# A local score bank's mask as two 64-column products, and pieces of row transposes and gate at other places of the attention steps

## The chip, the cores and the metric

The kernel runs on one core of one Trainium2 chip. Its five engines (TensorE, VectorE, ScalarE, GpSimd and SyncE; PE, DVE, ACT, POOL and SP in the profile) each work through a list of instructions of their own, in order, and wait for each other with semaphores. The metric is the device time of one execution in microseconds. Before the change three runs gave 695.32, 699.48 and 699.75 us, with a median of 699.48 us.

## The reference

The reference is window attention over 8 batches and 8 heads, and a mixture of experts over its output rows. A sequence has 32 global and 512 local positions with 64 numbers per head. Global queries see all 544 keys; a local query sees the 32 global keys and the local keys at most 32 positions away.

```
s_g = scale * q_g @ k_all.T ;  out_g = sm(s_g) @ v_all
s_ll = where(|pos_q - pos_k| <= 32, scale * q_l @ k_l.T, -1e9)
a_l  = sm(concat([scale * q_l @ k_g.T, s_ll]))
out_l = a_l @ concat([v_g, v_l])
x = concat([out_g, out_l]) with the heads side by side: 8 x 576 rows of 512
for each row in order: e = argmax(x @ w_gate), or the row before's e if sigmoid(x @ w_local) >= 0.5
out = softmax(x @ w_gate)[e] * (relu(x @ w1[e]) @ w2[e])
```

## The kernel before

The attention comes first and takes about the first 243 us of the profiled execution. Two heads (a pair) are worked on together. `run` walks over 48 units, six for each batch, in the order local pair 0, local pair 1, global 0, local pair 2, global 1, local pair 3. The step of a unit `nx` does its scores, and the transposes and the value product of the unit two steps earlier, `st`. So a step is one of six kinds, by the kinds of `nx` and `st`; they come round once a batch:

- `nx` local 0, `st` global 1 of the batch before
- `nx` local 1, `st` local 3 of the batch before
- `nx` global 0, `st` local 0
- `nx` local 2, `st` local 1
- `nx` global 1, `st` global 0
- `nx` local 3, `st` local 2

A local unit has two score banks (`hb` 0 and 1), each one PSUM bank of 128 x 512. `l_s` fills a bank: one bf16 product of the identity with a table (`mask`) writes 0 or -8e9 into 256 of its columns, then eight fp32 products add the scores (L243). Each of these eight has 64 stationary columns, and they write rows 0 to 63 and rows 64 to 127 of the bank by turns. `l_max` (VectorE, L248 and L250) takes the row maximum and writes the difference into `pe`, `l_exp` (ScalarE, L254) makes its exponential, `l_t` (L260) transposes it on TensorE with ScalarE copying it out (L262), and `l_av` (L276) multiplies it with the values in products of 32 stationary columns. `g_s`, `g_max`, `g_exp`, `g_t` and `g_av` do the same for a global unit.

TensorE thus works with three shapes of its stationary operand: 128 columns (every transpose, and the mask product), 64 columns (L243 and the global scores L296) and 32 columns (`l_av`, `g_av` L339, the gate products L367, L375, L388). The profile writes them as 128*128, 128*64 and 128*32.

The rest of a batch is a list of pieces, `fin`, of which `fpiece` does one: `f1` (four transposes L352 of a finished 128 columns of the attention output, copied to `xT` by ScalarE, L353), `f1g` (the same for the global rows, L359), `f2` and `f2g` (gate products), `f3` (transposes of the gate). A step calls `fpiece` at two places. The pieces due are the same in every batch from the second on: in the step of local 0 it is `f1` of pair 2 of the batch before, in that of local 1 its `f1g`, in that of global 0 its `f2g` and the `f1` of its pair 3, in that of local 2 its `f2` and `f3`, in that of global 1 `f1` of this batch's pairs 0 and 1, and in that of local 3 none.

Buffers that matter here: score banks are a ring of four PSUM banks (ps0 to ps3), transposes of all kinds go through a ring of two (ps4 and ps5, `ps_t`), value and gate products through another ring of two (ps6 and ps7, `ps_o`). The program order is the order of the code; no scheduler moves anything. Between the pieces of VectorE's work `drip` puts single instructions of the routing (`keys`, `probs`, `stage_a`).

After the attention come `tail` and the experts (`Moe`), which the change doesn't touch: the products L1251 and L1262 over weights loaded by SyncE, in the order of the experts.

Of the kernel before, what the change touches and what calls it, by code (L numbers as in the profile page):

```python
# [18 lines left out]
P = 128  # L19
# [80 lines left out]
class Attn:  # L100
# [125 lines left out]
    def l_s(self, st, hb):  # L226
        nc = self.nc
        if hb == 0:
            b, pr = st["u"]
            if pr == 0:  # L230
                self.cur[b]["xa"] = self.xa()
                self.cur[b]["xg"] = self.xg()
            st["pe"] = self.pe()
        qbd = st["qbd"]
        kf = st["kx"].rearrange("p m c k -> p (m c k)")
        sp = st["sp"] = self.bank(self.ps_s)
        mo = sp.rearrange("p t (k c) -> p t k c", c=32)[:, :, 0::3, :]
        nc.tensor.matmul(mo, self.cst.idb, self.mask[:, 4 * hb:4 * hb + 4], start=True, stop=False, skip_group_check=True)
        for t in range(4):
            for t2 in range(2):  # L240
                w = 8 * hb + 2 * t + t2
                f = 32 * (3 * (w // 2) + w % 2)
                nc.tensor.matmul(sp[64 * t2:64 * t2 + 64, t], qbd[:, w], kf[:, f:f + P], start=False, stop=True, skip_group_check=True)  # L243
# [176 lines left out]
    def run(self, rt, moe):  # L420
        order = []
        for b in range(B):
            order += [("l", b, 0), ("l", b, 1), ("g", b, 0), ("l", b, 2), ("g", b, 1), ("l", b, 3)]
        units = [{"k": k, "u": (b, i)} for k, b, i in order]
        pairs = [u for u in units if u["k"] == "l"]
        n = len(units)
        fin = []
        when = []

        def fpiece():  # L430
            if fin and when[0] <= s:
                f, a = fin.pop(0)
                when.pop(0)
                if f is not None:
                    f(*a)
        nc = self.nc
        for k in range(2):
            self.load(*pairs[k]["u"])
        self.load_g(0)
        self.loadv(*pairs[0]["u"])  # L440
        self.cst.ident()
        warm = self.ps_o()[:, 0:P]
        for _ in range(8):
            nc.tensor.matmul(warm, self.cst.idf, self.cst.idf, start=True, stop=True)
        nc.gpsimd.memset(self.pg.t[0], 0.0)
        self.blank(0)
        self.make_mask()
        self.prep(pairs[0])
        self.blank(1)
        nc.vector.memset(self.pg.t[1], 0.0)  # L450
        npr, late = 0, None
        for s in range(n):
            nx = units[s]
            st = units[s - 2] if s >= 2 else None
            nl = nx["k"] == "l"
            sl = st is not None and st["k"] == "l"
            sg = st is not None and not sl
            if nl:
                if npr + 2 < len(pairs):
                    b, i = pairs[npr + 2]["u"]  # L460
                    self.load(b, i)
                    if i == 0:
                        self.load_g(b)
                if npr + 1 < len(pairs):
                    self.loadv(*pairs[npr + 1]["u"])
                npr += 1
                if npr < len(pairs):
                    self.prep(pairs[npr])
            if sl:
                self.l_t(st, 0)  # L470
                self.l_t(st, 1)
            if sg:
                self.g_t(st)
            if late is not None:
                self.l_exp(late, 1)
                late = None
            if nl:
                self.l_s(nx, 0)
                self.l_max(nx, 0)
            else:  # L480
                self.g_s(nx)
                self.g_max(nx)
            fpiece()
            if sl:
                self.l_av(st, 0)
            if nl:
                self.l_exp(nx, 0)
                self.l_s(nx, 1)
                self.l_max(nx, 1)
            fpiece()  # L490
            if not nl:
                self.g_exp(nx)
            if sl:
                self.l_av(st, 1)
            if sg:
                self.g_av(st)
            if nl:
                if s in DEFER:
                    late = nx
                else:  # L500
                    self.l_exp(nx, 1)
            if s == 0:
                self.cst.load()
                self.cst.rest()
                self.gens += [self.setup(), rt.setup()]
            if s < 6:
                self.drip(4)
            moe.pre(s - n)
            if st is not None:
                b, i = st["u"]  # L510
                if sl:
                    fin.append((self.f1, (b, i)))
                    if i == 3:
                        fin += [(self.f2, (b,)), (self.f3, (b, rt))]
                elif i == 1:
                    fin += [(self.f1g, (b,)), (None, ()), (self.f2g, (b,))]
            if len(fin) > 4:
                fpiece()
            when += [s + 1] * (len(fin) - len(when))
        self.drip(1000)  # L520
        moe.tail = self.tail(units[n - 2], units[n - 1], fin, rt, moe)
# [1049 lines left out]
```

## Time and profile before

| | us |
|---|---|
| median of three runs | 699.48 |
| profiled execution | 698.19 |
| its span, first to last instruction | 696.5 |
| TensorE busy (share of the span) | 671.7 (96%) |
| VectorE busy | 427.4 (61%) |
| ScalarE busy | 342.6 (49%) |
| GpSimd busy | 196.2 (28%) |
| mean granted TensorE clock | 0.990 |

The profiled execution is one run of its own, with 1.7 us around its span. A row of the timeline has the start and the length of a run of equal instructions on one engine, both in us, then engine, line, operation, what is written and read, the shape, and the count. TensorE's products are pipelined: a product's row is longer than the time after which the next one may start, so rows overlap, and costs are read from starts. PEld is the loading of a stationary operand, which can go on beside products.

### The profile page before, as it was taken

To read this page: it belongs to the slowest core of one execution; us is meant where nothing else is said; L and a number is where in the kernel's file an instruction comes from. 1 tells how busy PE (TensorE), PEld (TensorE's weight loads), DVE (VectorE), ACT (ScalarE), POOL (GpSimd) and SP (SyncE) were. 2 spreads that over 40 slices of the span, in tenths; PEclk is the share of its full clock that TensorE was granted. 3 is DMA by queue.
4 is the path that set the end of the run, shared out by engine and by line. 5 is a ranking of instruction groups with operands and counts; after the bars stand their busy time and mean duration, and the time that the engine had idled before them with its cause. 6 is when DMAs were issued, how large, how long until landed. Compare 5 with 4: busy or idle time off the path is not lost.

```text
span 696.5 us, 18391 instructions
## 1 busy us (share of the span) xinstructions
PE 671.7 (96%) x7253; PEld 564.2 (81%) x7253; DVE 427.4 (61%) x1057; ACT 342.6 (49%) x614; POOL 196.2 (28%) x321
## 2 busy tenths in 40 slices
PE   9999999999899899998997999999999999999995
PEld 7777777777677787897886898889898989888994
DVE  7878777678887777995516645426353516345563
ACT  4555555655454674652326535334444425255563
POOL 7634344243333301032013303031304021032033
PEclk9999999999999999999999999999999999999998
DMA  8956967866846497776517666428385417265673
GB/s 331 387 213 238 353 235 274 311 240 226 309 181 262 140 353 247 257 230 238 191 60 257 200 219 200 145 76 257 126 260 158 159 66 235 67 211 179 234 259 112
DMA packets 43014, 151.46 MB, mean 217 GB/s; under 512 B 7965, under 2 KB 9245, under 8 KB 38688
## 3 DMA queue, kind: packets, MB, share of 16 engines
q1 hardware_dynamic: 35536, 126.92, 51.5%
q0 software_dynamic: 6960, 21.90, 9.8%
q8 instruction: 77, 1.26, 0.7%
q14 instruction: 153, 1.25, 0.5%
q10 hardware_dynamic: 288, 0.13, 0.1%
HBM read 130.55 MB, written 19.69 MB: 216 GB/s over the span
## 4 chain that ended last, share of the span: by engine, by line
PE 59%; DVE 3%; issue 1%; ACT 1%; POOL 0%; DVEq 0%; ACTq 0%; POOLq 0%
PE ps L1262 28%; PE ps L1251 26%; PE ps L1205 3%; DVE wp L1160 1%; DVE wq L1160 1%; PE ps L1374 0%; DVE xT L991 0%; PE ps L999 0%; POOL xa L1191 0%; DVE xT L989 0%; DVE hl L1254 0%; DVE wp L1208 0%; PE ps L276 0%; PE ps L1363 0%; DVE xl L1160 0%
## 5 line engine op out<-in xcount | busy, mean ns | idle before, releaser
L1268 POOL DMA_INDIRECT out_dram<-y,tk x39 | 40.5, 1039 | 320.0 <-ACT y L1267 257.0
L1262 PE MATMUL ps<-wp,wq 128*128 128x512 f32 x504 | 128.0, 401 | 0.9 <-ACT wq L1365 0.9
L1262 PEld LDWEIGHTS ps<-wp,wq 128*128 128x128 f32 x504 | 93.2, 190 | 20.5 <-ACT wq L1365 1.1
L1251 PE MATMUL ps<-wp,wp 128*128 128x256 f32 (+6 forms) x672 | 107.8, 320 | 0.0
L1251 PEld LDWEIGHTS ps<-wp,wp 128*128 128x128 f32 x672 | 103.4, 189 | 3.6
L1254 DVE SCALAR_TENSOR_TENSOR wq<-ps,wq 128x256 fp32r<-128x256 f32 (+6 forms) x80 | 41.3, 519 | 71.8 <-ACT wq L1253 71.6
L191 POOL TENSOR_SCALAR_AFFINE_SELECT qbd<-raw 64x512 f32<-64x512 f32 x62 | 44.6, 719 | 119.5 <-PE ps L243 100.6
L1208 DVE TENSOR_TENSOR wp<-ps,wp 128x512 fp32r<-128x512 f32 x40 | 27.4, 690 | 80.0 <-ACT wp L1207 80.0
L1253 ACT ACTIVATE wq<-ps 128x256 fp32r<-128x256 f32 (+6 forms) x80 | 36.8, 463 | 77.3 <-PE ps L1251 69.6
L243 PE MATMUL ps<-kx,qbd 128*64 128x128 f32 x1024 | 71.4, 281 | 1.8 <-issue 1.7
L243 PEld LDWEIGHTS ps<-kx,qbd 128*64 128x64 f32 x1024 | 55.1, 137 | 12.7 <-issue 8.3
L1267 ACT ACTIVATE y<-ps,pp 128x512 f32<-128x512 f32 x39 | 26.9, 689 | 76.4 <-PE ps L1262 70.8
L248 DVE TENSOR_REDUCE mx<-ps 128x4 f32<-128x512 f32 x64 | 43.9, 686 | 29.3 <-PE ps L243 29.3
L1160 DVE TENSOR_TENSOR wp<-raw,wp 128x1024 fp32r<-128x1024 f32 x47 | 56.9, 1216 | 2.5 <-ACT wp L1150 2.5
L254 ACT ACTIVATE pe<-pe 128x512 f32<-128x512 f32 x64 | 40.7, 636 | 32.9 <-DVE pe L250 32.9
L1191 POOL DMA_INDIRECT xa<-xs,idx x42 | 51.3, 1220 | 17.1 <-issue 10.0
L1150 ACT CAST wp<-raw 128x1024 fp32r<-128x1024 f32 x49 | 50.7, 1045 | 1.3 <-DMA raw<-in_w_dram 0.5
L1207 ACT CAST wp<-ps 128x512 fp32r<-128x512 f32 x40 | 23.4, 588 | 55.4 <-PE ps L1205 55.4
L250 DVE TENSOR_TENSOR pe<-ps,mx 128x512 f32<-128x512 f32 x64 | 44.0, 688 | 1.6
L276 PE MATMUL ps<-v,pt 128*32 128x65 f32 x2048 | 42.7, 222 | 2.1 <-DVE xa L284 0.8
L276 PEld LDWEIGHTS ps<-v,pt 128*32 128x32 f32 x2048 | 33.3, 110 | 13.8 <-issue 6.7
L191 POOL TENSOR_SCALAR_AFFINE_SELECT kx<-raw 128x384 f32<-128x384 f32 (+3 forms) x127 | 42.7, 369 | 3.0 <-DMA raw<-in_qk_dram 0.9
(279 smaller groups left out, 1173.0 us busy)
## 6 DMA issues: line engine op xcount, KB each, us to landing
raw<-in_w_dram SPq DMA_DIRECT2D x78, 512.0 KB, 3.9
v<-in_vw_dram SPq DMA_DIRECT2D x32, 1040.0 KB, 9.9
raw<-in_qk_dram SPq DMA_DIRECT2D x32, 528.0 KB, 8.2
xa<-in_w_dram SPq DMA_DIRECT2D x26, 512.0 KB, 5.0
xT<-in_w_dram SPq DMA_DIRECT2D x20, 512.0 KB, 4.1
xs<-xa SPq DMA_DIRECT2D x8, 1056.0 KB
qgb<-in_qg_dram SPq DMA_DIRECT2D x8, 128.0 KB
xa<-xs,idx POOLq DMA_INDIRECT x42
```

Source lines behind the costliest of these rows:

```text
L191: self.nc.gpsimd.affine_select(out=out, in_=in_, pattern=pat, compare_op=ALU.is_ge, fill=0.0, base=0, channel_multiplier=0)
L243: nc.tensor.matmul(sp[64 * t2:64 * t2 + 64, t], qbd[:, w], kf[:, f:f + P], start=False, stop=True, skip_group_check=True)
L248: nc.vector.tensor_reduce(out=mx, in_=st["sp"], axis=AX.X, op=ALU.max)
L250: nc.vector.tensor_tensor(out=st["pe"][:, 4 * hb:4 * hb + 4], in0=st["sp"], in1=mx.broadcast_to([P, 4, P]), op=ALU.subtract)
L254: self.nc.scalar.activation(out=pe, in_=pe, func=AF.Exp, scale=SCALE)
L276: nc.tensor.matmul(o[32 * w4:32 * w4 + 32, g, h], pt[:, 2 * g + w4 // 2, w4 % 2, h, :], v[:, w, h * (D + 1):(h + 1) * (D + 1)], start=True ...
L1150: nc.scalar.copy(out=hi, in_=raw)
L1160: (nc.gpsimd if pool else nc.vector).tensor_tensor(out=lo, in0=raw, in1=hi.bitcast(F32), op=ALU.subtract)
L1191: self.nc.gpsimd.indirect_dma_start(out=self.xr[j] if k == "early" else self.xr4[:, j], out_offset=None, in_=src, in_offset=bass.IndirectO ...
L1251: nc.tensor.matmul(ph, a[:, dc, fs], b_[:, dc, n0:n1], start=(n == 0), stop=(n == 11))
L1254: nc.vector.scalar_tensor_tensor(out=hl[:, fc, n0:n1], in0=ph, scalar=0.0, in1=hh[:, fc, n0:n1].bitcast(F32), op0=ALU.max, op1=ALU.subtract)
L1262: nc.tensor.matmul(py, a[:, fc, js], b_[:, fs], start=(fc == 0 and k == 0), stop=(fc == 7 and k == 2))
```

## The change

The mask product becomes two products, one with columns 0 to 63 of the identity into rows 0 to 63 of the bank, the other with columns 64 to 127 into rows 64 to 127. Each has 64 stationary columns and moves the same 256 columns of the table. `fpiece` keeps its two calls per step; where they stand now depends on the kinds of `nx` and `st`.

```diff
         mo = sp.rearrange("p t (k c) -> p t k c", c=32)[:, :, 0::3, :]
-        nc.tensor.matmul(mo, self.cst.idb, self.mask[:, 4 * hb:4 * hb + 4], start=True, stop=False, skip_group_check=True)
+        for r in (slice(0, 64), slice(64, P)):
+            nc.tensor.matmul(mo[r], self.cst.idb[:, r], self.mask[:, 4 * hb:4 * hb + 4], start=True, stop=False, skip_group_check=True)
...
             else:
                 self.g_s(nx)
                 self.g_max(nx)
-            fpiece()
+            if sl:
+                fpiece()
+            if not nl:
+                fpiece()
             if sl:
                 self.l_av(st, 0)
             if nl:
                 self.l_exp(nx, 0)
                 self.l_s(nx, 1)
                 self.l_max(nx, 1)
-            fpiece()
+            if nl:
+                fpiece()
+                if sg:
+                    fpiece()
             if not nl:
+                if sg:
+                    fpiece()
                 self.g_exp(nx)
```

For the steps with `nx` and `st` both local, or both global, the order of the pieces is the same as before. It differs in two of the six kinds of steps. The diff adds lines, so line numbers behind it are one or more higher in the changed kernel (L238 is L239, L243 is L244, L352 is L353).

In the step of local 0, on TensorE, where the third batch begins, there stood this before (ps1 and ps2 are the unit's two score banks, xa1 the attention output of the batch before, ptg1 the transposed global part):

```order
L328 MATMUL ps4_67<-idf_81,pg1_149 128x128 x3
L238 LDWEIGHTS idb_82
L238 MATMUL ps1_64<-mask_154,idb_82 128x4x2x32
L243 MATMUL ps1_64<-kx0_146,qbd0_144 64x128 x8
L352 MATMUL ps5_68<-idf_81,xa1_109 128x128 x4
L238 LDWEIGHTS idb_82
L238 MATMUL ps2_65<-mask_154,idb_82 128x4x2x32
L243 MATMUL ps2_65<-kx0_146,qbd0_144 64x128 x8
L339 MATMUL ps7_70<-v1_133,ptg1_151 32x65 x2
```

And this stands at the same place in the changed kernel:

```order
L329 MATMUL ps4_67<-idf_81,pg1_149 128x128 x3
L239 LDWEIGHTS idb_82
L239 MATMUL ps1_64<-mask_154,idb_82 64x4x2x32
L239 LDWEIGHTS idb_82
L239 MATMUL ps1_64<-mask_154,idb_82 64x4x2x32
L244 MATMUL ps1_64<-kx0_146,qbd0_144 64x128 x8
L239 LDWEIGHTS idb_82
L239 MATMUL ps2_65<-mask_154,idb_82 64x4x2x32
L239 LDWEIGHTS idb_82
L239 MATMUL ps2_65<-mask_154,idb_82 64x4x2x32
L244 MATMUL ps2_65<-kx0_146,qbd0_144 64x128 x8
L353 MATMUL ps5_68<-idf_81,xa1_109 128x128 x4
```

The transposes of `f1` have moved from between the unit's two score banks to behind the second one; the two banks now follow each other. The same moves ScalarE's copy of these transposes. Before, from this step into the next (pe2 is the new unit's score tile, pt2 and pt3 the next step's transposed scores):

```order
L329 COPY ptg1_151<-ps4_67 128x384
L254 ACTIVATE pe1_138<-pe1_138 128x512
L353 COPY xT_112<-ps5_68 128x512
L254 ACTIVATE pe2_139<-pe2_139 128x512
L262 COPY pt2_142<-ps4_67 128x512
L262 COPY pt3_143<-ps5_68 128x512
```

And in the changed kernel:

```order
L330 COPY ptg1_151<-ps4_67 128x384
L255 ACTIVATE pe1_138<-pe1_138 128x512
L255 ACTIVATE pe2_139<-pe2_139 128x512
L354 COPY xT_112<-ps5_68 128x512
L263 COPY pt2_142<-ps4_67 128x512
L263 COPY pt3_143<-ps5_68 128x512
```

The copy to `xT` now stands behind the exponential of the new unit's first bank, and it still frees ps5 for the second four transposes of the next step. Seven batches have this step with an `f1`. In the step of global 0, on TensorE, before (xgT1 feeds the global gate product, v3 the values):

```order
L296 MATMUL ps2_65<-raw1_78,qgb0_152 64x288
L375 MATMUL ps6_69<-xgT1_117,wgg_84 32x32 x4
L276 MATMUL ps7_70<-v3_135,pt0_140 32x65 x16
L352 MATMUL ps5_68<-idf_81,xa1_109 128x128 x4
L276 MATMUL ps6_69<-v3_135,pt1_141 32x65 x16
```

And in the changed kernel:

```order
L297 MATMUL ps2_65<-raw1_78,qgb0_152 64x288
L376 MATMUL ps6_69<-xgT1_117,wgg_84 32x32 x4
L353 MATMUL ps5_68<-idf_81,xa1_109 128x128 x4
L277 MATMUL ps7_70<-v3_135,pt0_140 32x65 x16
L277 MATMUL ps6_69<-v3_135,pt1_141 32x65 x16
```

Here `f1` has moved ahead of both value products. VectorE, GpSimd and SyncE have the same instructions in the same order as before.

## The prediction

> **What bounds the kernel now.** I read the page's first lines, then busy times by stretches of the attention stage, where the whole change lies.
>
> ```profile
> span 696.5 us, 18391 instructions
> PE 671.7 (96%) x7253; PEld 564.2 (81%) x7253; DVE 427.4 (61%) x1057; ACT 342.6 (49%) x614; POOL 196.2 (28%) x321
> ```
>
> ```profile
> 11.00:50.00 39.00, 38.15 (x791) 28.61 (x790) 31.44 (x109) 22.51 (x51) 21.23 (x62) 1.00 0.80 315
> 50.00:100.00 50.00, 50.00 (x1069) 38.52 (x1071) 37.38 (x129) 29.47 (x69) 19.32 (x42) 1.00 0.72 259
> 100.00:150.00 50.00, 49.99 (x1064) 38.32 (x1057) 38.45 (x131) 27.70 (x63) 20.42 (x44) 1.00 0.77 287
> 150.00:200.00 50.00, 47.12 (x952) 34.88 (x952) 40.41 (x147) 26.34 (x63) 15.53 (x35) 1.00 0.65 234
> 200.00:240.00 40.00, 36.12 (x726) 28.31 (x729) 32.59 (x110) 21.53 (x47) 16.22 (x24) 1.00 0.63 230
> ```
>
> After the stretch's length come busy us of PE, PEld, DVE, ACT and POOL, then granted clock and DMA. From 50 to 150 us TensorE is busy for 99.99 of 100 us at full clock: it is the bound. From 150 on it idles some 7 us in 90, and VectorE, now with routing between its pieces, is at 81%. What TensorE saves before 150 us moves everything later forward; after 150 us only part will.
>
> Busy isn't useful, though. The timeline of TensorE around one local step shows what a mask product costs.
>
> ```profile
> 88.63 1.09 PE L260 MATMUL ps<-idf,pe 128*128 128x128 f32 x8
> 89.56 0.27 PE L238 MATMUL ps<-mask,idb 128*128 128x256 bf16 x1
> 89.76 1.09 PE L243 MATMUL ps<-kx,qbd 128*64 128x128 f32 x16
> 90.78 0.33 PE L359 MATMUL ps<-idf,xg 128*128 128x128 f32 x1
> 91.04 0.67 PE L276 MATMUL ps<-v,pt 128*32 128x65 f32 x32
> 91.64 0.28 PE L238 MATMUL ps<-mask,idb 128*128 128x256 bf16 x1
> 91.85 1.09 PE L243 MATMUL ps<-kx,qbd 128*64 128x128 f32 x16
> ```
>
> The same rows cut finer give the rates: two narrow looks at the start of the scores, one at their end, and one at a last pair.
>
> ```profile
> 91.85 0.33 PE L243 MATMUL ps<-kx,qbd 128*64 128x128 f32 x2
> 91.85 0.44 PE L243 MATMUL ps<-kx,qbd 128*64 128x128 f32 x4
> 91.85 0.55 PE L243 MATMUL ps<-kx,qbd 128*64 128x128 f32 x6
> ...
> 92.34 0.61 PE L243 MATMUL ps<-kx,qbd 128*64 128x128 f32 x8
> 92.88 0.26 PE L276 MATMUL ps<-v,pt 128*32 128x65 f32 x4
> ...
> 169.78 0.28 PE L243 MATMUL ps<-kx,qbd 128*64 128x128 f32 x2
> ```
>
> Score products go in pairs, one for each half of the rows, 0.11 us per pair (0.44 to 0.55). The last four pairs start at 92.34, 92.45, 92.56 and 92.67. The last has streamed by 92.78, and the next work, of 32 columns, starts at 92.88: a **change of shape costs 0.10 us** (0.094 where I use more digits). The first pair after a change takes 0.33 us against 0.28 for a last one: the first load of a stationary operand can't go ahead of the change, and **0.05 us of load lies bare**. Within one shape neither is paid: the eight transposes from 88.63 and the mask behind them, all of 128 columns, take 0.93 us, which is 8 x 0.11 and one bare load.
>
> The mask product itself streams for about 0.11 us: 256 columns of L1251 take 0.119 (11.40 us for 96, below), and between the mask at 91.64 and the scores at 91.85 lie 0.21, of which 0.10 is the change.
>
> ```profile
> 666.11 11.40 PE ps L1251 x96
> L238 PEld LDWEIGHTS <-idb x64: 95/97/151, 4.8 to 231.6; 128*128 128x128 bf16 x64
> L243 PEld LDWEIGHTS ps<-kx,qbd x1024: 132/137/232, 5.4 to 232.6; 128*64 128x64 f32 x171
> ```
>
> **The change part by part.** I count changes of shape and bare loads; 64 masks in all.
>
> *Mask as two products.* Score pairs run at once (two records of 0.27 end within 0.28), so I take two mask products side by side for the same 0.11 us. Bounds of this term: 0 to +0.11 us for each mask, if they ran one after the other; I take 0, by the nearest row, the score pairs.
>
> 1. Masks behind transposes (L260 or L328), as at 89.56: 30 of 64, the first bank of nearly every unit. Before: mask, change, scores with a bare load. After: change, mask with a bare load, scores. The sum is the same: 0. Bounds: the bare load is of bf16, not f32; between -0.05 and +0.05 each.
> 2. Masks behind `l_av`, as at 91.64: the second bank of each unit whose step has a local `st`, 3 x 8 - 1 = 23. Before: change to 128, mask, change to 64, bare load 0.05, and 0.01 of the mask's own (its row is 0.28 here, 0.27 at 89.56). After: one change, one bare load 0.05. Saved 0.094 + 0.012 = 0.106 us each: **2.4 us**.
> 3. Masks behind `f1` in the step of local 0: seven. Before 64, 128, 64, 32 from the first scores to `g_av`, three changes with two bare loads on the way in; with `f1` moved behind both banks 64, 128, 32. One change and one bare load less: 0.148 each, **1.0 us**.
> 4. The first two units have four banks one after the other, so three masks lose two changes each (0.2 us). Two of these come ahead of a wait for GpSimd's copies in the second unit: the scores from 8.48 take 1.36 us instead of 1.09. GpSimd isn't faster, so only the last counts: **0.2 us**.
>
> ```profile
> 8.48 1.36 PE L243 MATMUL ps<-kx,qbd 128*64 128x128 f32 x16
> 9.98 1.09 PE L243 MATMUL ps<-kx,qbd 128*64 128x128 f32 x16
> ```
>
> *The moved `f1` of local 0's step has a price on ScalarE.* Its copy (0.59 us) now stands behind the exponential of the new first bank, which waits for VectorE, and the next step's second four transposes need the bank that this copy frees. Rows for the third, first and sixth passage between batches:
>
> ```profile
> 86.78 0.59 ACT L353 COPY xT<-ps 128x512 f32<-128x512 f32 x1 [0.81 <-PE ps L352]
> 87.61 0.63 ACT L254 ACTIVATE pe<-pe 128x512 f32<-128x512 f32 x1 [0.24 <-DVE pe L250]
> ...
> 31.70 0.63 ACT L254 ACTIVATE pe<-pe 128x512 f32<-128x512 f32 x1 [0.94 <-DVE pe L250]
> ...
> 32.02 1.09 PE L260 MATMUL ps<-idf,pe 128*128 128x128 f32 x8
> ...
> 172.99 0.63 ACT L254 ACTIVATE pe<-pe 128x512 f32<-128x512 f32 x1 [1.03 <-DVE pe L250]
> ...
> 173.22 1.09 PE L260 MATMUL ps<-idf,pe 128*128 128x128 f32 x8
> ...
> 171.11 1.27 DVE L824 TENSOR_TENSOR_SCAN sc<-z,sc,ps 5x512 f32<-5x512 f32 x1
> ```
>
> The second four transposes start 0.49 us after the first (0.05 and four times 0.11). Usually the copy would end at 87.61 + 0.63 + 0.59 = 88.83, and they start at 88.63 + 0.49 - 0.15 = 88.97: no wait, with 0.14 to spare. At the passage at 32 us the copy would end at 32.92 against 32.36, a wait of 0.56; at 173 us, behind a long scan on VectorE, 174.21 against 173.56, 0.65. Together **1.2 us lost**. Bounds: 0, if VectorE comes earlier by as much, to 2.2, if the 0.14 is used up too and the other five wait 0.2.
>
> *The moved `f1` of global 0's step* leaves three changes as before (64, 32, 128, 32 against 64, 32, 128, 32).
>
> ```profile
> 95.56 0.27 PE L375 MATMUL ps<-xgT,wgg 128*32 128x32 f32 x8
> 95.65 0.64 PE L276 MATMUL ps<-v,pt 128*32 128x65 f32 x32
> 96.22 0.66 PE L352 MATMUL ps<-idf,xa 128*128 128x128 f32 x4
> 96.81 0.67 PE L276 MATMUL ps<-v,pt 128*32 128x65 f32 x32
> ...
> 94.86 0.42 DVE L284 TENSOR_TENSOR xa<-ps,rs 128x256 f32<-128x256 f32 x1
> ...
> 96.33 0.18 DVE L377 COPY gsb<-ps 128x32 f32<-128x32 f32 x1
> ```
>
> Its input is written by 95.28 and it would start about 95.75; the last value product needs the bank that VectorE's gate copy frees at 96.51 and starts at 96.81. Cover of 0.3 to 0.5 us; cost 0. If VectorE fell half a microsecond further behind, each would wait.
>
> *Sum.* 2.4 + 1.0 + 0.2 - 1.2 = 2.4 us. Eight of the 23 and two of the seven lie after 150 us, 1.1 us of gain; I count half of it as lost to VectorE's pace: 0.5. That leaves **1.9 us**. The experts aren't touched and follow when the attention ends. The profiled execution took 698.19 us, so 696.3, 0.5% under the median of 699.48; that median is itself near the top of runs that spread over 4.4 us.
>
> *A rule weighed.* The mask's load is now the fast one: 128 columns of bf16 in 97 ns against 137 for 64 of f32. The Trainium skill (TensorE: Matmul & The Clock Gate, Weight-path perf modes) says that fast weight load applies only to 128 weights of a type other than fp32, and the same page puts a load at columns / 1.2 ns, an estimate of 53 ns for 64. By that, case 1 saves nothing, as I have it.
>
> **The rivals.**
>
> - *The two mask products run one after the other* (the slower side). Price 64 x 0.11 = 7.0 us, and 696.3 + 7.0 = 703.3. It decides from about 1.9 / 64 = 0.03 us a mask on. For it: no bf16 product of 64 columns stands in this trace. Against it: pairs of L243 take 0.28 together, and four 32-column products of L276 go the same way (32 in 0.60 us). I give it 8 in 100. The Trainium skill (the same page, Part 3, The mechanism) has a rule that would bring this about, that a load overlaps running products only where the row group differs; both halves use all rows. The L243 pairs speak against that rule.
> - *The gain goes into waits.* VectorE's pace after 150 us takes all of the 1.1, the ScalarE copy costs 2.2, or the second mask's load lies bare (0.05 x 64 = 3.2): 697.7 to 699.5. For it: idle TensorE after 150 us and 0.14 us to spare. 25 in 100.
> - *Bare bf16 loads are short.* The mask's bare load was 0.01 with 128 columns; if it stays so with 64, every mask saves up to 0.04 more, 64 x 0.04 = 2.6, and 693.7. For it: half as much data. Against it: the longer f32 row. 15 in 100.
> - *The forecast*, 694.5 to 697.7: 48 in 100. What is left, 4, is a clock that drops at other places than now.
>
> **How the numbers follow.** The likeliest case gives 696.3. The range takes in the short loads and the waits, and on the low side the spread of the runs: 692.5 to 700.0; it leaves out the serial products. A measurement of this kernel tells 1% (7 us) from no change, that is 692.5 and 706.5. Below 692.5 only the short loads with a low run: 0.08. Above 706.5 only the serial products with a high run: 0.03. Within: 0.89.
>
> **What would show it.** Two L239 rows starting together with the scores 0.11 us behind them show the pair at once; a gap of 0.2 or more the serial rival. Behind `l_av` the time from its end to the scores' end must fall by 0.1. The scores' first pair should take 0.28, not 0.33. The step of local 0 should be 0.15 us shorter, except at the first and sixth passage, where L261 waits for ScalarE's L354. The attention should end 2 us earlier and the experts take as long as before. I am wrong if the scores' first load stays bare behind the mask, or if VectorE's waits grow in every batch.

## The result and the profile after

The changed kernel takes 692.86 us in the median of 22 runs, the kernel before 697.83 us in 22 runs beside it. The ratio is 0.9939, with a 95% interval of 0.992 to 0.9958: 2.9 to 5.6 us less. The means are 4.2 us apart. The profiled execution of the changed kernel took 695.93 us, one of its slower ones, 2.26 us under the one shown of before.

The page of the changed kernel begins so:

```profile
span 694.2 us, 18512 instructions
PE 667.4 (96%) x7317; PEld 565.9 (82%) x7317; DVE 428.2 (62%) x1057; ACT 342.2 (49%) x614; POOL 196.0 (28%) x321
```

TensorE has 64 products and 64 loads more and is busy 4.3 us less; the other engines do the same work as before. All of the 2.3 us that the span is shorter have been won when the attention ends: the first L1262 starts at 252.88 us before and at 250.59 after (there L1271), and the experts follow with the same rows.

The second bank of a local step, TensorE's timeline of the changed kernel, first whole, then its start alone, then the loads of the same moment:

```profile
90.01 0.36 PE L277 MATMUL ps<-v,pt 128*32 128x65 f32 x12
90.29 0.30 PE L239 MATMUL ps<-mask,idb 128*64 128x256 bf16 x2
90.43 1.04 PE L244 MATMUL ps<-kx,qbd 128*64 128x128 f32 x16
91.39 0.26 PE L277 MATMUL ps<-v,pt 128*32 128x65 f32 x4
...
90.43 0.28 PE L244 MATMUL ps<-kx,qbd 128*64 128x128 f32 x2
...
90.29 0.11 PEld L239 LDWEIGHTS <-idb 128*64 128x64 bf16 x2
90.32 0.25 PEld L244 LDWEIGHTS ps<-kx,qbd 128*64 128x64 f32 x4
```

The two mask products together take 0.30 us, and the scores start 0.14 us behind them: they run at once. The first pair of scores takes 0.28, no longer 0.33, and the sixteen 1.04, no longer 1.09. Their load starts 0.03 us behind the mask's. From the mask's start to the next value product it is now 1.10 us; before, from 91.64 to 92.88, it was 1.24.

The step of local 0 in the same batch, first before (with the row of VectorE that `f1` waits for), then after:

```profile
84.00 0.88 PE L328 MATMUL ps<-idf,pg 128*128 128x128 f32 x6
84.71 0.27 PE L238 MATMUL ps<-mask,idb 128*128 128x256 bf16 x1
84.92 1.09 PE L243 MATMUL ps<-kx,qbd 128*64 128x128 f32 x16
85.94 0.80 PE L352 MATMUL ps<-idf,xa 128*128 128x128 f32 x4
86.58 0.27 PE L238 MATMUL ps<-mask,idb 128*128 128x256 bf16 x1
86.78 1.09 PE L243 MATMUL ps<-kx,qbd 128*64 128x128 f32 x16
87.81 0.89 PE L339 MATMUL ps<-v,ptg 128*32 128x65 f32 x48
...
85.84 0.41 DVE L284 TENSOR_TENSOR xa<-ps,rs 128x256 f32<-128x256 f32 x1
```

```profile
82.98 0.88 PE L329 MATMUL ps<-idf,pg 128*128 128x128 f32 x6
83.79 0.30 PE L239 MATMUL ps<-mask,idb 128*64 128x256 bf16 x2
83.92 1.04 PE L244 MATMUL ps<-kx,qbd 128*64 128x128 f32 x16
84.80 0.28 PE L239 MATMUL ps<-mask,idb 128*64 128x256 bf16 x2
84.91 1.04 PE L244 MATMUL ps<-kx,qbd 128*64 128x128 f32 x16
85.88 0.66 PE L353 MATMUL ps<-idf,xa 128*128 128x128 f32 x4
86.46 0.89 PE L340 MATMUL ps<-v,ptg 128*32 128x65 f32 x48
```

From the global transposes to `g_av` it is 3.81 us before and 3.48 after. The second mask follows the first bank's scores within one shape, with no change and no bare load (0.11 us to its scores). And `f1` before takes 0.80 us for four transposes that take 0.66 after: its third transpose starts at 86.31, behind VectorE's division that ends at 86.25, so it waited for its input.

Measured in this way, from the first transposes of one step to those of the next, most steps of the quiet batches (50 to 150 us) repeat within 0.01 to 0.02 us, and a kernel's steps can be set side by side. A few are longer: those with a standstill (see below the table) and single others, such as the changed kernel's step of local 0 at 140 us, with 4.49. The table has the usual values, in us:

| step (`nx`, `st`) | before | mask pair alone | moves alone | whole change |
|---|---|---|---|---|
| local 0, global 1 | 4.63 | 4.60 | 4.59 | 4.30 |
| local 1, local 3 | 4.85 | 4.68 | 4.85 | 4.71 |
| global 0, local 0 | 3.93 | 3.93 | 3.93 | 3.93 |
| local 2, local 1 | 6.08 | 5.91 | 6.08 | 5.91 |
| global 1, global 0 | 3.72 | 3.72 | 3.72 | 3.72 |
| local 3, local 2 | 4.59 | 4.42 | 4.59 | 4.42 |
| a batch | 27.80 | 27.26 | 27.76 | 26.99 |

The whole change saves 0.81 us in a usual quiet batch. Eight such batches would be 6.5 us, and the profiled execution shows 2.3. A good part of the difference stands in rows of this kind, the loads of TensorE in the changed kernel, at three places:

```profile
30.12 0.14 PEld L244 LDWEIGHTS ps<-kx,qbd 128*64 128x64 f32 x2 [1.52 <-issue]
...
117.92 0.20 PEld L277 LDWEIGHTS ps<-v,pt 128*32 128x32 f32 x9 [0.85 <-issue]
...
131.38 0.37 PEld L277 LDWEIGHTS ps<-v,pt 128*32 128x32 f32 x18 [1.39 <-issue]
```

TensorE stands still, mostly in the middle of a run of equal products, and "issue" says that it waits for nothing that the profile shows. Of over 0.3 us there are five such standstills, 4.9 us in all (from one start to the next), in the attention of the changed kernel's profiled execution, and two, 2.3 us, in that of before. When I count all of TensorE's records together (loads, products and its few semaphore and branch instructions), each of the seven lies at number 193 plus a multiple of 256 (961, 1217, 4801, 5057 and 5313; before 1217 and 7617). So they lie at the borders of blocks of 256. And one queue of the page carries such blocks:

```profile
q8 instruction: 78, 1.28, 0.8%
```

These are packets of 16,384 bytes, which is 64 bytes for each of 256 records. Each of the standstills ends 1.2 to 1.6 us after such a packet landed. I read them as waits for TensorE's own instructions.

The one near 28.6 us shows what the pair has to do with it. In the kernel before, the last packet ahead of the border at record 961 lands at 28.64 us, and TensorE reaches that border at 30.0 and goes on without a standstill. In the changed kernel the packet lands at 28.59, but TensorE is at the border at 28.58 already and goes on at 30.12. By then the pair has added 16 records (18 mask products and their loads instead of 10), so the same number stands earlier in the program. The row of the kernel before has only the 0.21 us that stand ahead of these loads at other changes of shape too (at 89.76, for one):

```profile
30.17 0.31 PEld L243 LDWEIGHTS ps<-kx,qbd 128*64 128x64 f32 x6 [0.21 <-issue]
```

### The profile page after: what moved, and what is told of

Read it like the earlier page. It is cut to its first block, busy times and chain, and to the rows that moved or that the text cites. A ratio compares the mean times of both kernels' runs of the same rounds, so it can differ in the third digit from the quotient of the medians.

```text
span 694.2 us, 18512 instructions
## 1 busy us (share of the span) xinstructions
PE 667.4 (96%) x7317; PEld 565.9 (82%) x7317; DVE 428.2 (62%) x1057; ACT 342.2 (49%) x614; POOL 196.0 (28%) x321
## 4 chain that ended last, share of the span: by engine, by line
PE 59%; DVE 3%; issue 1%; ACT 1%; POOL 0%; ACTq 0%; DVEq 0%; POOLq 0%
PE ps L1271 28%; PE ps L1260 26%; PE ps L1214 3%; DVE wp L1169 1%; DVE wq L1169 1%; PE ps L1383 0%; PE ps L1008 0%; DVE xT L1000 0%; POOL xa L1200 0%; DVE xT L998 0%; ACT wp L1159 0%; DVE hl L1263 0%; DVE wp L1217 0%; PE ps L277 0%; ACT hh L1262 0%
## 5 line engine op out<-in xcount | busy, mean ns | idle before, releaser
L1271 PE MATMUL ps<-wp,wq 128*128 128x512 f32 x504 | 127.9, 401 | 0.9 <-ACT wq L1374 0.9
L1271 PEld LDWEIGHTS ps<-wp,wq 128*128 128x128 f32 x504 | 93.2, 190 | 20.5 <-ACT wq L1374 1.1
L1262 ACT ACTIVATE wq<-ps 128x256 fp32r<-128x256 f32 (+6 forms) x80 | 36.8, 463 | 77.4 <-PE ps L1260 67.6
L244 PE MATMUL ps<-kx,qbd 128*64 128x128 f32 x1024 | 67.5, 275 | 1.3 <-issue 1.3
L244 PEld LDWEIGHTS ps<-kx,qbd 128*64 128x64 f32 x1024 | 58.8, 138 | 2.0 <-issue 1.5
```

The costliest lines, as they stand in the source:

```text
L1271: nc.tensor.matmul(py, a[:, fc, js], b_[:, fs], start=(fc == 0 and k == 0), stop=(fc == 7 and k == 2))
```

## The experiments

My theory A was that the mask pair saves what the table says, and that the moved `f1` saves a wait for VectorE and a change of shape. Theory B gave all of the gain to the shape, theory C to the moves. Theory D was about the standstills: that a block of instructions comes late because its load queues behind data.

**The pair alone.**

```diff
-        nc.tensor.matmul(mo, self.cst.idb, self.mask[:, 4 * hb:4 * hb + 4], start=True, stop=False, skip_group_check=True)
+        for r in (slice(0, 64), slice(64, P)):
+            nc.tensor.matmul(mo[r], self.cst.idb[:, r], self.mask[:, 4 * hb:4 * hb + 4], start=True, stop=False, skip_group_check=True)
```

> The kernel before with the mask as two products; fpiece stands where it stood. Theory A (sizes read from the trace of the changed kernel): a mask behind transposes saves 0.03 us, one behind the value product 0.137, so 30 x 0.03 + 23 x 0.137 + 7 x 0.03 + 0.2 = 4.4 us less until the end of the attention, less what TensorE waits for its instructions; 3 to 4.5 us less in the time. Theory B (all of the gain is from the shape, the moved pieces are worth nothing): as much as the whole change, 4.3 to 5. Theory C (the moves carry it): under 2.

Measured 692.98 us against 698.55, ratio 0.9931 (0.9904 to 0.9959), 4.8 us. The attention ends at 248.29 us, 4.6 earlier, with 1.6 us of standstills. The pair alone is as fast as the whole change; theory C falls. The time can't choose between theory B and theory A, whose 3 to 4.5 us lie in the interval; the steps of the table do that.

**The moves alone** (the kernel before with the change's `fpiece` calls).

> The kernel before with the new places of fpiece, the mask as one product. Theory A: f1 in the step of local 0 no longer waits for VectorE (0.09 to 0.15 us in four batches, 0.3 in the first, 0.95 in the last, together about 2.0) and one change of shape less in seven steps (0.7), against waits of the next step's transposes of 0.5 us: 2 us less. Theory B: 0.7 us less or nothing, because the wait comes back at another place. Theory C: 3 us or more.

Measured 696.69 us, ratio 0.9963 (0.9942 to 0.9984). By its steps theory A is wrong here: a step of local 0 is only 0.04 us shorter. The rows, from the second mask on:

```profile
86.63 0.28 PE L238 MATMUL ps<-mask,idb 128*128 128x256 bf16 x1
86.84 1.09 PE L243 MATMUL ps<-kx,qbd 128*64 128x128 f32 x16
87.87 0.66 PE L352 MATMUL ps<-idf,xa 128*128 128x128 f32 x4
88.45 0.66 PE L339 MATMUL ps<-v,ptg 128*32 128x65 f32 x32
```

`f1` waits no more (0.66), but with a mask of 128 columns the banks' succession is 64, 128, 64 and then `f1` brings 128 again: a change more than before, which eats the 0.14. The move is worth its 0.3 us only together with the pair. Without its standstills the attention ends at 250.64 us, before at 250.60. So the 1 to 4 us in the time don't show in this execution's attention, and I can't say where they come from.

**The change without the move in the step of global 0** (there the second `fpiece` stands behind `l_av` again).

> The whole change without the move in the step of global 0. All theories that count changes of shape: the same time as the whole change, 0.993 to 0.994 of before, since that step took 1.842 us from the gate product to its end in both traces. If that move is worth something by itself (exponentials of the global unit earlier on ScalarE), this is over 1 us slower than the whole change.

Measured 693.01 us, ratio 0.9932 (0.9907 to 0.9958): that move is worth nothing that can be measured, as its usual step of 3.93 us in the kernel before, in this one and in all columns of the table says.

**Both banks first in the steps with two local units too.**

```diff
+            if nl:
+                self.l_exp(nx, 0)
+                self.l_s(nx, 1)
+                self.l_max(nx, 1)
             if sl:
                 fpiece()
...
             if sl:
                 self.l_av(st, 0)
-            if nl:
-                self.l_exp(nx, 0)
-                self.l_s(nx, 1)
-                self.l_max(nx, 1)
...
+            if s >= 30:
+                self.drip()
```

> The whole change, and in the steps with both units local the second score bank also stands right behind the first, ahead of the pieces and of both value products; one more routing instruction per step from step 30 on. Changes of shape per batch fall by five (two in local 1 and local 3, one in local 2), 0.094 each, and bare loads by five of 0.027: 0.6 us a batch, 4.8 us in eight. Theory A: 3 to 4.8 us less than the whole change, 8 to 9 less than before. Rival: VectorE, which then has four passes over score banks in a row (2.8 us) ahead of the value products' divisions, makes value products and f1 wait: no gain over the whole change, or a loss of up to 5.

Measured 701.3 us, ratio 1.004 (1.0013 to 1.0067): slower, and the attention ends at 259.5 us. The step of local 3, which has no pieces, gains 0.26 us (4.16 against 4.42), where two changes of shape and two bare loads count 0.24. That of local 1 loses 0.28 (4.99 against 4.71) and that of local 2 loses 0.54. The rows of the latter, from `f2` on:

```profile
98.37 1.07 PE L368 MATMUL ps<-xT,wgl 128*32 128x512 f32 x8
99.25 0.64 PE L277 MATMUL ps<-v,pt 128*32 128x65 f32 x32
100.14 0.66 PE L386 MATMUL ps<-idf,gsb 128*128 128x128 f32 x4 [0.25 <-ACT gsb L369]
100.72 0.23 PE L389 MATMUL ps<-sel,gsb 128*32 128x9 f32 x2
101.11 0.66 PE L277 MATMUL ps<-v,pt 128*32 128x65 f32 x32 [0.16 <-DVE L L391]
```

The gate's transposes now wait for ScalarE's copy of the product right ahead of them, and the value product for VectorE. From 160 us on four steps take 2.3 to 3.4 us longer than in the changed kernel. Which part of that is VectorE's four passes and which the added routing instructions wasn't separated.

**Without most value loads.** Three kernels (before, pair alone, whole change) with this edit:

```diff
-        nc.sync.dma_start(v.rearrange("p w c -> p (w c)"), self.vw[b, pr])
+        if self.v.k <= NV:
+            nc.sync.dma_start(v.rearrange("p w c -> p (w c)"), self.vw[b, pr])
```

> The kernel before, with only the first five value tiles loaded (the pairs from the sixth on take one of these): 27 of 32 value loads are left out, about 28 MB of transfers. The values differ, and with them the routing and the experts' work, so only the end of the attention is compared (the first product L1262, at 252.9 us in the profiled execution before). Theory D (TensorE stands still where a block of its instructions comes late, because the block's load queues behind data): the standstills with nothing to wait for at 35.5, 144.6 and 189.8 us are gone, none over 0.1 us is left at those block borders, and the attention ends about 2.3 us earlier, near 250.6. Rival (blocks come late for another reason, such as the time at which they are asked for): standstills of 0.3 to 1.5 us remain.

> The mask as two products alone, with the same 27 value loads left out; only the end of the attention is compared. Theory D: no standstill at a block border; the end comes 4.2 to 4.8 us before that of the kernel before without these loads, by 22 steps of 0.166 and about 0.03 for the other first banks.

> The whole change with the same 27 value loads left out; only the end of the attention is compared. Theory D: no standstill at a block border, so the moved f1 shows what it is worth: 0.3 us in each of the five quiet steps of local 0, 5.5 to 6.5 us in all against the kernel before without these loads, 1 to 2 more than the pair alone. Rival (the moves are worth nothing because VectorE sets the pace behind them): the same end as the pair alone within 0.4.

Each was executed once. The attention ends at 250.45, 248.55 and 246.85 us, and the standstills at borders are 0.6, 1.3 and 1.6 us. Taken off, that is 249.8, 247.3 and 245.3: the pair gains 2.5 us, the moves on top of it 2.0. So both ends come less early than was expected (1.9 and 3.6 us, or 2.5 and 4.5 without standstills, where 4.2 to 4.8 and 5.5 to 6.5 were expected), and only the difference between them is in theory A's 1 to 2. The pair's quiet steps are those of the table, but in the stretch with the routing work, after 150 us, steps of it wait longer than before (the sixth step of local 1 takes 7.33 us against 6.76). Single executions scatter here: with all loads, and standstills taken off, the attention of the pair ends at 246.7 and, in a second execution further on, 245.8, that of the whole change at 245.7 and 244.3. The moves thus gain 1.0, 1.5 and 2.0 us in three pairs of executions.

Theory D isn't settled by this. DMA engines of the changed kernel are 24 to 44% busy from 30 us on instead of 70 to 77%, and of its standstills after 30 us (four in its profile) none is left. But the kernel before has a new one, of 0.6 us at 83 us, which theory D ruled out. With all its loads the pair has none after 30 us either (in its second execution one, at 35), and the changed kernel in its second execution none after 36 us. The one near 28.6 us is there in the pair and in the change, where the first five value loads still run. Its surroundings, in the changed kernel with all its loads (PE busy, four engines more, clock 1.00, DMA share, GB/s):

```profile
11.00:20.00 9.00, 8.73 (x196) 6.68 (x194) 7.71 (x20) 5.96 (x15) 5.94 (x25) 1.00 0.96 360
20.00:30.00 10.00, 8.85 (x191) 6.81 (x189) 8.69 (x38) 6.14 (x15) 7.40 (x20) 1.00 1.01 415
30.00:60.00 30.00, 29.71 (x656) 23.58 (x660) 23.01 (x80) 16.29 (x38) 11.93 (x26) 1.00 0.73 274
```

**Value loads in halves**, the second issued by ScalarE at the end of the step:

```diff
-        nc.sync.dma_start(v.rearrange("p w c -> p (w c)"), self.vw[b, pr])
+        f, h = v.rearrange("p w c -> p (w c)"), NW * VW // 2
+        nc.sync.dma_start(f[:, 0:h], self.vw[b, pr][:, 0:h])
+        self.rest = (f[:, h:], self.vw[b, pr][:, h:])
+        if not paced:
+            nc.sync.dma_start(*self.rest)
+            self.rest = None
...
+            if self.rest is not None:
+                nc.scalar.dma_start(*self.rest)
+                self.rest = None
```

> The whole change, with each value load cut in two halves; from the third unit on the second half is issued by ScalarE at the end of the step and not by SyncE together with the first. Theory D: less data stands ahead of an instruction block, standstills at block borders fall from 4.6 us in the profiled execution of the change to under 2, and the time is 1 to 3 us under the whole change, 0.990 to 0.992 of before. Rival: the transfers are as many bytes as before and the borders hit them as often: the same as the whole change, 0.993 to 0.995.

Measured 691.33 us, ratio 0.9911 (0.9878 to 0.9944), with 3.6 us of standstills in its profile. The time is where theory D has it, the standstills are not (under 2).

**Four kernels side by side**, on one chip with the same runs of before (median 696.06 us).

> The changed kernel as it is, once more, to see whether its long standstills at block borders stand at the same places in another execution. Theory D (the transfers' timing decides which border is late): the one near 28.5 us, behind 10 us of full DMA engines, is there again with 1.2 to 1.6 us; those at 117, 123 and 130 us are not, or elsewhere; the attention ends at 247 to 250 us instead of 250.6. Rival (places fixed by the program): the same five. Time 0.992 to 0.996 of before.

> The mask as two products alone, once more, beside the whole change on the same chip. If the moves are worth nothing on top of it: within 1 us of the whole change. If they are worth the 0.3 us that each quiet step of local 0 shows: the whole change 1 to 2 us faster than this.

> The whole change with halved and paced value loads, once more, beside the whole change on the same chip. Theory D: 1 to 2.5 us under the whole change. Rival: the same within 1 us, and the 0.9911 of its first comparison was the draw of few runs.

> The mask as two products alone, with halved and paced value loads. If pacing and the pair are independent, as much under the pair alone as the paced change is under the change; if pacing helps only where TensorE is ahead of its blocks, less.

| kernel | median us | ratio (95% interval) | standstills in the profile, us | attention ends, us |
|---|---|---|---|---|
| whole change | 689.04 | 0.9902 (0.9872 to 0.9932) | 2.0 | 246.28 |
| pair alone | 690.08 | 0.9920 (0.9892 to 0.9949) | 1.7 | 247.54 |
| change, paced loads | 689.53 | 0.9912 (0.9880 to 0.9944) | 3.9 | 248.69 |
| pair, paced loads | 689.07 | 0.9905 (0.9872 to 0.9937) | 3.2 | 249.74 |

No two of these can be told apart. Pacing doesn't remove standstills, and the 0.9911 above was not a gain over the change. None of the versions beats the changed kernel beyond doubt. The standstills of this second profiled execution of the changed kernel lie at 22.4, 28.6 and 35.2 us; those at 117, 123 and 130 us are gone. So the same program meets them at other places in another execution, and only those near 28.6 and 35 us are in both. The one near 28.6 us took 1.0 us, less than the 1.2 to 1.6 expected; the attention ended earlier than expected too, and the ratio is below the 0.992 named. The loads around that one:

```profile
27.93 0.68 PEld L244 LDWEIGHTS ps<-kx,qbd 128*64 128x64 f32 x11
29.58 0.14 PEld L244 LDWEIGHTS ps<-kx,qbd 128*64 128x64 f32 x2 [0.97 <-issue]
```

The spans differ by more than the attention does. Between the two executions of the changed kernel it ends 4.3 us earlier and the span is 8.0 us shorter; most of the rest goes with the granted clock. The first, then the second:

```profile
core 0: 694.2 us, clock 0.990
```

```profile
core 0: 686.2 us, clock 0.996
```

In the trace's record of the clock, the first has three stretches of 3.4 us at half clock between 318 and 386 us, the second has one, at 367 us. Product by product, the second is ahead by 4.3 us until 315 us and by 7.75 from 392 us on, so the other 3.4 us arise in this stretch.

## Why the prediction was right or wrong

The range held the time, though only by 0.36 us at its lower end, and the direction and the mechanism were right: changes of shape were the price, and the mask pair saves them. The sum was too small: 1.9 us forecast, 4.2 measured between the means of 22 runs. The time is nearest to my rival of the short bare load (693.7), and the range held it because it had taken that rival in. That the profiled execution shows 2.26 is luck, two errors that cancel there: the kernel gains more than I said, and that execution loses more in a place that I didn't look at.

- **TensorE bounds the attention, and what it saves moves everything forward.** Right: from 50 to 150 us most steps differ from before by the same amounts in every batch.
- **Side by side, 0 for the second product.** Right, 0.30 us for both. The Trainium skill (TensorE: Matmul & The Clock Gate, Part 3, The mechanism) has the rule that a load overlaps running products only where the row group differs. The trace disagrees: the loads of L244 start at 90.32 us, while both mask products run (90.29 to 90.59), and all of these use all 128 rows.
- **A bare load of 0.05 us for the mask.** Mis-sized: it is 0.03, since from the mask to the scores it is 0.14 us behind a change and 0.11 without one. I set the short load aside as a rival; it is right by some two thirds. Each of the 30 masks of case 1 thereby saves 0.03 instead of 0, and each of the 23 of case 2 some 0.14 instead of 0.106. The steps with both units local show the two together, 0.17 against a forecast of 0.11. The same page of the Trainium skill puts a load at columns / 1.2 ns, an estimate of 53 ns for 64 columns; that is what lies bare of an f32 load here (0.05 us), but of this bf16 load only 0.03 us do.
- **The moved `f1` of local 0, 0.15 us a batch.** Mis-sized: 0.33. I didn't see that `f1` waited 0.14 us for VectorE at its old place (0.80 against 0.66 us) and counted only the shape. What the pair and the move save there doesn't add up from each alone: 0.03 and 0.04, together 0.33. The moves alone show why: with the old mask the moved `f1` costs one change of shape more.
- **Its price on ScalarE, 1.2 us.** Near in size, 1.5 us, but from other terms: nothing at the first passage instead of 0.56, 0.47 at the sixth instead of 0.65, and 0.94 at the seventh, where I had none. At the first the next step takes 4.68 us in the change without value loads, as in the pair alone: no wait. In the quiet batches 0.03 us (4.71 against 4.68). At the sixth the long scan on VectorE holds it as forecast, TensorE and ScalarE of the changed kernel:

```profile
172.72 0.66 PE L261 MATMUL ps<-idf,pe 128*128 128x128 f32 x4
173.68 0.66 PE L261 MATMUL ps<-idf,pe 128*128 128x128 f32 x4 [0.30 <-ACT xT L354]
...
173.06 0.57 ACT L354 COPY xT<-ps 128x512 f32<-128x512 f32 x1
```

  From four transposes to the next four it is 0.96 us where 0.49 is usual: 0.47 us of waiting.
- **After 150 us half of 1.1 us is lost.** What is left came out (0.6 forecast, 0.7 measured), the terms did not. The steps from 159 us on sum to 81.8 us before, its standstill taken off, and to 81.1 after, 0.7 less. At the sizes of the quiet steps, seven second banks and two moves would have saved 7 x 0.17 + 2 x 0.33 = 1.85 us there, so 1.1 is lost and not 0.5. The seventh passage shows where such a gain goes. Before, `f1` waits there 0.95 us for VectorE; after, 0.4, and then the next step waits 0.94 for ScalarE. Before, then after:

```profile
203.43 0.44 PE L352 MATMUL ps<-idf,xa 128*128 128x128 f32 x2
204.65 0.44 PE L352 MATMUL ps<-idf,xa 128*128 128x128 f32 x2 [0.78 <-DVE xa L284]
```

```profile
203.36 0.44 PE L353 MATMUL ps<-idf,xa 128*128 128x128 f32 x2 [0.27 <-DVE xa L285]
203.72 0.89 PE L340 MATMUL ps<-v,ptg 128*32 128x65 f32 x48
204.54 0.66 PE L261 MATMUL ps<-idf,pe 128*128 128x128 f32 x4
205.98 0.66 PE L261 MATMUL ps<-idf,pe 128*128 128x128 f32 x4 [0.78 <-ACT xT L354]
```

- **The move in the step of global 0, 0.** Right, 3.93 us in all columns of the table.
- **What the forecast lacked:** the standstills at block borders. They took 2.3 us of the execution that I read, in rows of "issue" that I passed over, and 4.9 us of the changed kernel's profiled execution, but 2.0 in its second one. With 2.6 us more of them, a gain of 4.9 shows as 2.3. Of the 2.6, the standstill near 28.6 us (1.55) belongs to the pair: all versions with it have one there, of 0.6 to 1.6 us, and those without it have none. The rest changes from one execution to the next. That a faster TensorE also meets more of them elsewhere, as a block of 256 records lasts less long, was only argued.

## What to carry to other kernels

Where an engine is the bound and its steps repeat, compare step by step between two points that every version has: it gives hundredths of a microsecond where whole times scatter by several. Count changes of stationary shape over the whole succession of work, with the bare load behind each, since a move can be worth nothing alone and 0.3 us together with another edit. When a piece is moved, read first whether it waits where it stands now. And instructions that are added move the borders of an engine's blocks of instructions: here that cost 0.6 to 1.6 us at one border.

## What the runs showed of the hardware

As I read the traces, TensorE's instructions come in blocks of 256 records through the DMA engines (packets of 16,384 bytes), and at a border it may stand still for 0.3 to 1.6 us, with the block landed 1.2 to 1.6 us before it goes on. At the border at record 961 this happens in every version with the pair. The last packet ahead of it lands between 27.3 and 28.9 us in all versions. Those with the pair reach the border at 28.1 to 28.9 us and wait; the kernel before and the moves alone reach it at 29.6 to 30.1 and don't, though the DMA engines are as full ahead of it (a share of 1.02 from 20 to 28.6 us in both the kernel before and the changed one). Elsewhere the places change from one execution to the next. From 30 to 160 us a block's load starts 0.8 to 1.9 us behind the border before (medians) without most value loads and 1.8 to 2.9 us with them, so data in the queues may delay it, but single blocks come 4 to 7 us behind a border in both. One standstill came at 83 us with few loads, and cutting the loads in halves didn't lessen them: what else decides when a block comes is open.

A change between 128, 64 and 32 stationary columns costs 0.09 to 0.10 us beyond the streaming in the directions that the quiet batches of the kernel before show (128 to 64 or 32, 64 to 128 or 32, 32 to 128). Behind it, a product of 64 columns in bf16 leaves 0.03 us of load bare, one of 64 columns in f32 0.05.
